# Nyström attention and expert layer in one kernel: the last 64 tokens of a batch stored in two transfers, and a new table of order, banks and warming

## The chip, the cores and the metric

The kernel runs on one core of a Trainium2 chip. The metric is the time of one execution on the device in microseconds (us). Before the change the median of 3 runs is 426.99 us, the lowest 425.55 and the highest 430.17. The core has five engines that work side by side and wait for one another through semaphores: PE (matrix multiply, with its weight loads as a row of their own, PEld), DVE (vector), ACT (scalar and activation), POOL (GpSimd) and SP, which here only issues transfers. [...]

## What is computed

Per batch (8) and head (8) of 576 tokens of width 64: attention through 32 landmarks. The landmarks are means of 18 neighbouring tokens.

```
q_lm = q.reshape(B, H, m, S // m, D).mean(axis=3)
k_lm = k.reshape(B, H, m, S // m, D).mean(axis=3)
A = sm(q, k_lm);  Bm = sm(q_lm, k_lm);  C = sm(q_lm, k)
Z = Bm^T / (norm1(Bm) * norminf(Bm) + 1e-06)
for _ in range(6):
    Z = 2 * Z - Z @ Bm @ Z
return A @ Z @ C @ v
```

The result, as 4608 rows of 512, goes to a layer of 8 experts with one expert per token (`sm` above is a softmax; a token's expert is the largest of 8 cosine scores):

```
h = np.maximum(x[mask] @ w1[e], 0.0)        # 512 -> 1024
out[mask] = gate_w[mask, None] * (h @ w2[e])  # 1024 -> 512
```

## The kernel before, in words

The kernel works batch by batch, and several batches are under way at once. For a batch b: `loads` and `load_values` bring K, Q and V; `sums` adds 18 tokens to a landmark (wholly on DVE, or half on POOL, L668, and half on DVE, L671); `inverse` makes Bm (its first matmuls, `ps<-ksum,qsum`, need the sums of K and Q; its first DVE step is L700) and `powers` iterates Z (`ek`); `values` makes C and C v; `queries` and `scored` make A with a softmax whose subtraction and division are done in `both`, either on POOL (L953) or on DVE (L955); its last steps are the transpose L938 and the split of A into two float16 parts, L941 on ACT and L943 on DVE. The attention output itself is never formed: `landmarks` makes W = Z C v, `first_weights` multiplies w1 by W (`ps<-wstage,wt`), `scaled` splits that product into two float16 parts (`ww`, L1389 and L1391), and `first` multiplies A by it (`ps<-ab,ww`), so that one matmul chain gives the hidden layer. `hidden` takes the maximum with 0 and splits into two float16 parts (`ht`, ACT L1442 and DVE L1444, 16 pairs per batch). `second` multiplies by w2 (`ps<-w2c,ht`), whose two parts `second_weights` makes (norm by L1405 on ACT or L1407 on DVE; the parts by L1430 on DVE or L1432 on ACT, and L1434 on DVE). `outputs` scales by the gate (L1535 on ACT or L1533 on DVE) and stores.

A batch has 576 = 4 x 128 + 64 tokens. For the last 64 (c = 4) the two halves of the 512 columns lie in the two halves of the 128 partitions of `yt`, and one transfer stores both (L1542). The other chunks are stored by L1540.

Which expert a batch's weights are loaded for is decided by `guess` and `choose` from the landmarks (the DVE steps end in `gi`), and SP reads that number (L1291) before it issues the loads of w1 and w2 (L1311). The whole batch uses one expert; a general path behind a branch covers the case in which a token disagrees.

The order is written out by hand. All these functions are generators that ask for an engine, a buffer or a PSUM bank at each step. `Weave.run` goes through the table `TURNS`: each pair of characters names the generator that makes its next step now, and so fixes the order of the instructions on every engine. `CHOICES` says, where a step may go to one of two engines, which one; `BANKS` names the PSUM banks; `WARM` says at which turns a number of matmuls on ones, in units of 128 columns, is put into PE's stream (`keep_warm`, L591, up to 512 columns each), whose result nobody reads. SP's queue is in the same order, and each of its entries waits for its data before the next is issued.

Of the kernel before, what the change touches and what calls it, by code (L numbers as in the profile page):

```python
# [53 lines left out]
BUFS = dict(k=2, q=2, v=2, ek=4, u=3, ec=2, ct=2, ae=3, at=2, st1=4, st2=4, w2=6, ww=2, ht=12, ab=3, yt=3, land=3, wt=3)  # L54

TURNS = (
    "000006060606060b0b353333060000333c003c0100000001010707080836360136010101343h3g3g34343h010101343434343434013i01"
# [4 lines left out]
    "021m1n1n4l4l4n2m2m2m1m1m1m4p382m4i4o4q1m1m4r4g4q4m4s4n4o4p4n4n2m2m1m0n0n0t0t2n2n4s4r4u2n2n4u4g4n1m1m1m4k2m4k4k"
    "4t2n594t1n1n2n4d4k0o0o4m391o1o4b4b1m1m1m0259395a2n022n025a391o1o3902021n1n0202020202021o1o2n2n4g2n2n2n1n1n394g"
    "2n1p1p1p40405b5g5g5a5h5h5b5b5b5g2n2n5g1p4d4d3a3a5b2n2n2n2n2n2n0o0o3a2n2n2n2n5a5h5h5g5g3a5h1o1o5k5h5g5g3a3a5k3a"
    "5h2n2n3b3b3b3b3b5l5l5l5l5b5b5h5b1r5k1r1r1r1r5k2n5l5l2n4v2n2n2n2n5l5l5l5l5h2n1r030303035b2n1p5b5b5l5j5j5b030303"
    "0303032n032n5b03035b5b03030303035c5c03030303035b4d4d5g5g5g031p4d5b5b5b2n5b1p1p5b5b5b5n5n5n41411r5n412n411r5p5p"
    "2n2n41415c5n5h5h2n5n5n5g5h2n5m5m2n5j0j0j5q5q5q1r1p1p1q5q5q1r5n415n1p2n5g5h415n5n5n2n5s5s2n2n5t5t1r5s1r41415t2n"
    "5n5n5n5n1r1r1r2o2o5u5u2o0k0k5w5n4w4w4w5n5n5n5w411r1r5v5n5z5z5n5n60605v2o2o2o2o2o61631r612o2o2o66666161615p6367"
    "5u415y5y5y672o656464686363635y5y68695y424y4y1r1r69422o2o654y4y1r420p0p6a6a422o4y4y2o2o6d6c6d422o6d436e6c6e6d43"
    "436f6d0u0u4y4y2o2o6h436h6h6h6h6h6h1t1t432p2p2p4y1t1t43431t1t1s1s4444443y2o6j4y2p2p4x444x2p1s1s2p386f1r1r4y1r6k"  # L70
    "6k2o2o6m6l6l6k442p6m53536i531t1t6l1s1s6k2o6r6i6l1w6j6p6p526l6q6q6k3b6l6g6s6t6n6n6n6n6r416n6k1w1w2p2p2p2p6l1u0z"
    "0z2p2p2p2p2p2p2p6l6t5m6s2p2p2p2p6n6k6k6k6k6k6k6n6n6s6s1s1s4y6l441w2p6k6o6l6l6t6t6t4y6s0u0u6n2p2p6n4z6n1w6u6u2p"
    "1u10102p2p2p2p2p2p1w1u2p4z4z4z6g6o6l6l4z1w501u1u503b0q0q2p2p2p2p7373731u506u506g1u50502p2p501u1v1w6o741u74516o"
    "77776o4v1u1w741u2p2p2p2p2p2p1w2p2p7c7c3b1w1w1w1w7d7d1w7c1w1w2p2p6o55557d551w54547f7f7g7g552q2q2q2q2q7g7b7b5510"
    "105515157l7l7l1w1w7l7l5535557t762q7u7t7e7e7t2q2q552q515151517x7x7i2q2q7t7t7t7t7v7u7j1y1y7h511y1y1x1x7w7x2q7w7y"
    "2q2q2q80767i7j777h7y2q2q2r2r7f76802q2r2q2q81442q827v7k822q2q817k851w86211x1x7k837z1x1x2q877z2r2r7k8483842r2r2r"
# [1555 lines left out]
```

## Time and profile before

| what | us |
|---|---|
| median of 3 runs (lowest, highest) | 426.99 (425.55, 430.17) |
| the profiled execution, its own time | 429.22 |
| its span, first to last instruction | 427.4 |
| PE matmuls busy | 403.5 (94%) |
| DVE busy | 343.2 (80%) |
| ACT busy | 242.2 (57%) |
| POOL busy | 72.6 (17%) |
| DMA, mean rate | 182 GB/s |

The share of busy time is a union over instructions. A matmul's end is modelled, and matmuls overlap, so PE at 94% isn't PE at its peak: a gap between two matmuls that is shorter than one matmul's latency doesn't show. The chain of waits, followed back from the last instruction, says which engine held the end up at each moment.

### The profile page before, as it was taken

To read this page: it belongs to the slowest core of one execution; us is meant where nothing else is said; L and a number is where in the kernel's file an instruction comes from. 1 tells how busy PE (TensorE), PEld (TensorE's weight loads), DVE (VectorE), ACT (ScalarE), POOL (GpSimd) and SP (SyncE) were. 2 spreads that over 40 slices of the span, in tenths; PEclk is the share of its full clock that TensorE was granted. 3 is DMA by queue.
4 is the path that set the end of the run, shared out by engine and by line. 5 is a ranking of instruction groups with operands and counts; after the bars stand their busy time and mean duration, and the time that the engine had idled before them with its cause. 6 is when DMAs were issued, how large, how long until landed. Compare 5 with 4: busy or idle time off the path is not lost.

```text
span 427.4 us, 14590 instructions
## 1 busy us (share of the span) xinstructions
PE 403.5 (94%) x6105; PEld 244.8 (57%) x6105; DVE 343.2 (80%) x1009; ACT 242.2 (57%) x536; POOL 72.6 (17%) x74
## 2 busy tenths in 40 slices
PE   8877999899999999999999899999999999999995
PEld 3344654467654665457665467556755576457644
DVE  5698999888898999987997669984898579788630
ACT  1258657548568554675588436755566577546311
POOL 5131243400121205201242132301110020000100
PEclk9999999999999999999999899999999999999999
DMA  8699394040599359273595249500187105741012
GB/s 313 245 320 391 121 354 164 22 168 15 186 350 380 132 176 355 82 280 120 183 350 192 101 154 364 193 3 29 53 288 292 58 28 180 276 168 51 2 58 73
DMA packets 23705, 77.67 MB, mean 182 GB/s; under 512 B 2768, under 2 KB 6096, under 8 KB 21840
## 3 DMA queue, kind: packets, MB, share of 16 engines
q1 hardware_dynamic: 23344, 76.49, 49.9%
q8 instruction: 49, 0.80, 0.7%
q10 hardware_dynamic: 288, 0.18, 0.2%
q14 instruction: 24, 0.20, 0.1%
HBM read 61.92 MB, written 14.75 MB: 179 GB/s over the span
## 4 chain that ended last, share of the span: by engine, by line
PE 55%; DVE 39%; issue 4%; ACT 1%; POOL 0%; DVEq 0%; ACTq 0%; POOLq 0%
PE ps L505 50%; DVE ht L1444 5%; DVE w2c L1434 4%; PE ps L591 3%; DVE ksum L671 2%; DVE qsum L671 2%; DVE asum L932 2%; DVE am L926 2%; DVE cm L813 2%; DVE ae L955 1%; DVE ae L919 1%; DVE ww L1391 1%; DVE w2c L1430 1%; DVE ab L943 1%; DVE wsq L1407 1%
## 5 line engine op out<-in xcount | busy, mean ns | idle before, releaser
L505 PE MATMUL ps<-w2c,ht 128*128 128x512 f16 (+2 forms) x1176 | 200.6, 342 | 1.1 <-DVE yt L1533 0.6
L505 PEld LDWEIGHTS <-ht 128*128 128x128 f16 (+1 forms) x1176 | 95.4, 102 | 82.4 <-issue 6.2
L505 PE MATMUL ps<-ab,ww 128*128 128x288 f16 x768 | 103.6, 286 | 2.2 <-DVE ht L1444 1.0
L505 PEld LDWEIGHTS <-ww 128*128 128x128 f16 x768 | 73.7, 98 | 27.4 <-issue 6.6
L1442 ACT ACTIVATE ht<-ps 128x288 f16<-128x288 f32 x128 | 47.3, 410 | 36.7 <-PE ps L505 36.2
L1444 DVE SCALAR_TENSOR_TENSOR ht<-ps,ht 128x288 f16<-128x288 f32 x128 | 53.3, 447 | 3.2 <-ACT ht L1442 3.0
L1434 DVE SCALAR_TENSOR_TENSOR w2c<-wstage,wsc,w2c 128x1024 f16<-128x1024 f32 x32 | 42.1, 1317 | 0.4
L1197 ACT ACTIVATE junk<-ps 128x512 bf16<-128x512 f32 (+1 forms) x40 | 23.8, 594 | 31.5 <-DVE lg L1194 30.1
L1535 ACT ACTIVATE yt<-ps,gfac 128x512 f32<-128x512 f32 (+1 forms) x32 | 19.9, 630 | 28.6 <-PE ps L505 24.8
L1326 ACT ACTIVATE junk<-wstage 128x1024 bf16<-128x1024 f32 x32 | 33.7, 1055 | 0.5
L1215 POOL TENSOR_TENSOR nrm<-ssq,half 128x5 f32<-128x5 f32 x8 | 9.6, 1194 | 130.5 <-ACT junk L1197 130.5
L668 POOL TENSOR_TENSOR half<-q_t 128x576 f32<-128x576 f32 x13 | 20.1, 1543 | 55.8 <-DVE ksum L671 22.3
L1405 ACT ACTIVATE junk<-wstage 128x1024 bf16<-128x1024 f32 x22 | 23.2, 1056 | 2.8 <-DMA wstage<-w 2.6
L668 POOL TENSOR_TENSOR half<-k_t 128x576 f32<-128x576 f32 x11 | 16.2, 1471 | 50.4 <-DMA k_t<-kT 37.4
L1432 ACT ACTIVATE w2c<-wstage,wsc 128x1024 f16<-128x1024 f32 x21 | 24.0, 1148 | 0.3 <-DVE wsc L1416 0.3
L1389 ACT ACTIVATE ww<-ps,wsc 128x1024 f16<-128x1024 f32 (+1 forms) x18 | 17.5, 1014 | 9.9 <-DVE wsc L1339 5.8
L953 POOL TENSOR_TENSOR ae<-ae,am 128x576 f32<-128x576 f32 x10 | 12.5, 1257 | 55.2 <-DVE am L926 55.2
L505 PE MATMUL ps<-ek 32*32 32x64 f32 (+1 forms) x768 | 16.4, 215 | 5.3 <-DVE ek L1012 2.3
L1194 DVE TENSOR_REDUCE lg<-ps 128x8 f32<-128x64 f32 (+1 forms) x40 | 8.7, 218 | 15.5 <-ACT junk L1197 9.5
L1391 DVE SCALAR_TENSOR_TENSOR ww<-ps,wsc,ww 128x1024 f16<-128x1024 f32 (+1 forms) x18 | 20.5, 1153 | 0.7 <-ACT ww L1389 0.7
L591 PE MATMUL ps<-ones 128*128 128x512 bf16 (+3 forms) x70 | 18.4, 411 | 2.4 <-POOL ones L523 1.7
L505 PEld LDWEIGHTS ps<-ek 32*32 32x32 f32 x768 | 11.7, 105 | 13.6 <-DVE ek L1012 6.0
(215 smaller groups left out, 526.5 us busy)
## 6 DMA issues: line engine op xcount, KB each, us to landing
wstage<-w SPq DMA_DIRECT2D x64, 512.0 KB, 8.1
v<-v SPq DMA_DIRECT2D x16, 512.0 KB, 4.8
k_t<-kT SPq DMA_DIRECT2D x7, 1152.0 KB, 10.1
q_t<-qT SPq DMA_DIRECT2D x7, 1152.0 KB, 5.9
out<-yt SPq DMA_DIRECT2D x31, 256.0 KB, 3.7
abs__137<-ab SPq DMA_DIRECT2D x8, 576.0 KB, 3.1
k_t<-kT SPq DMA_DIRECT2D x2, 576.0 KB, 4.0
q_t<-qT SPq DMA_DIRECT2D x2, 576.0 KB
```

Of the source, the lines that this page charges most:

```text
L505: pe.matmul(o, lhsT, rhs, start=start, stop=stop)
L591: pe.matmul(warmth[:, 0:k * P], ones16, bc(ones16.unsqueeze(1), [P, k, P]), start=True, stop=True)
L668: pool.tensor_tensor(out=half, in0=sv[:, :, :, 0:9], in1=sv[:, :, :, 9:18], op=ALU.add)
L1197: act.activation(junk[lo:hi, 0:512].rearrange("p (j g x) -> p j g x", j=4, g=2), pfv[lo:hi, :, n, :, 0:D], AF.Square, accum_out=ssq[lo:hi, ...
L1326: act.activation(junk, stage[1, b, q], AF.Square, accum_out=sq[:, q:q + 1])
L1391: vec.scalar_tensor_tensor(out=ww[:, 1], in0=pw, scalar=sc, in1=ww[:, 0], op0=ALU.mult, op1=ALU.subtract)
L1405: act.activation(junk, stage[2, b, q], AF.Abs, accum_out=sq[:, q:q + 1])
L1432: act.activation(w[:, 0], st, AF.Copy, scale=sc)
L1434: vec.scalar_tensor_tensor(out=w[:, 1], in0=st, scalar=sc, in1=w[:, 0], op0=ALU.mult, op1=ALU.subtract)
L1442: act.activation(ht[:, 0, r], ph[:, 0:HS], AF.Relu)
L1444: vec.scalar_tensor_tensor(out=ht[:, 1, r], in0=ph[:, 0:HS], scalar=0.0, in1=ht[:, 0, r], op0=ALU.max, op1=ALU.subtract)
L1535: act.activation(yt[:, 0:n], py[:, cols], AF.Copy, scale=fac)
```

## The change

Two things are changed. The store of the last 64 tokens is issued as two transfers of 64 rows of 256 columns. And the tables `TURNS`, `CHOICES`, `BANKS` and `WARM` are replaced; of these only `WARM` can be read.

```diff
-WARM = {1: 33, 19: 136, 36: 6, 46: 7, 108: 13, 126: 5, 134: 30, 192: 27, 225: 5}
+WARM = {4: 32, 23: 91, 59: 6, 79: 7, 153: 10, 190: 8, 211: 6}
...
         if c < 4:
             (act if last else sp).dma_start(out[t0:t0 + P, cols], yt[:, 0:n])
         else:
-            sp.dma_start(out[t0:t0 + 64].rearrange("t (s x) -> s t x", s=2), yt[:, 0:256])
+            for s in range(2):
+                sp.dma_start(out[t0:t0 + 64, 256 * s:256 * s + 256], yt[64 * s:64 * s + 64, 0:256])
```

The instructions stay the same but for the engine that `CHOICES` names, the stores and the warming. Counted in the order of instructions, before and after (two small copies, L877 and L1075, change by one each as well):

| step | before | after |
|---|---|---|
| softmax subtraction and division on DVE (L955) / on POOL (L953) | 13 / 19 | 6 / 26 |
| norm of w2 on DVE (L1407) / on ACT (L1405) | 10 / 22 | 6 / 26 |
| first part of w2 on DVE (L1430) / on ACT (L1432) | 11 / 21 | 8 / 24 |
| output of 512 columns on DVE (L1533) / on ACT (L1535) | 7 / 24 | 11 / 20 |
| C v on DVE (L855) / on ACT (L859, two each) | 6 / 4 | 3 / 10 |
| turned C, 512 columns, on DVE / on ACT (L874) | 5 / 11 | 3 / 13 |
| copies of the iteration, pairs of batches, on DVE (L1010) / on ACT (L1008) | 8 / 7 | 4 / 11 |
| warming matmuls, all sizes (L591) | 70 | 42 |

The first place is on PE, at the start of the program, where the warming run `ps<-ones_90` stands ahead of the first matmuls of `inverse(0)` (`ps<-ksum,qsum`) and of `values(0)` (`ps<-k_t,qsum`). Before, the run between `e_142` and `ksum,qsum` has 34 matmuls of 512 columns; its first and last rows:

```order
L505 MATMUL ps<-e_142,ones 128x64
L591 LDWEIGHTS ones_90
L591 MATMUL ps<-ones_90 128x512
...
L591 MATMUL ps<-ones_90 128x512
L505 MATMUL ps<-ksum,qsum 32x32 x8
L505 MATMUL ps<-k_t,qsum 32x288 x16
L591 LDWEIGHTS ones_90
L591 MATMUL ps<-ones_90 128x512
```

In the changed kernel the same run has 22 matmuls of 512 columns and one of 384:

```order
L505 MATMUL ps<-e_142,ones 128x64
L591 LDWEIGHTS ones_90
L591 MATMUL ps<-ones_90 128x512
...
L591 MATMUL ps<-ones_90 128x384
L505 MATMUL ps<-ksum,qsum 32x32 x8
L505 MATMUL ps<-k_t,qsum 32x288 x16
L505 LDWEIGHTS v_123
```

So the same matmuls stand behind 11.25 fewer warming matmuls of 512 columns, and the next short warming run, behind `k_t,qsum`, is gone.

The second place is on DVE, where the softmax of A for the second batch is made, among other steps. Before:

```order
L926 TENSOR_REDUCE am<-ae 128x18
L955 TENSOR_TENSOR ae<-ae,am 128x576
L836 RECIPROCAL cfac<-cfac 128x2
L839 TENSOR_TENSOR cfac<-cfac,rct 128x2
L1194 TENSOR_REDUCE lg_103<-ps 128x8
L671 TENSOR_REDUCE ksum<-half 128x64
L926 TENSOR_REDUCE am<-ae 128x18
L955 TENSOR_TENSOR ae<-ae,am 128x576
L932 TENSOR_REDUCE asum<-ae 128x18
```

In the changed kernel the subtractions of this softmax stand on POOL, between halves of the sums (`half`) and the power of the norms (`nrm`):

```order
L953 TENSOR_TENSOR ae<-ae,am 128x576
L668 TENSOR_TENSOR half<-k_t 128x576
L668 TENSOR_TENSOR half<-q_t 128x576 x2
L1215 TENSOR_TENSOR nrm<-ssq,half_115 128x5
L668 TENSOR_TENSOR half<-q_t 128x576
L953 TENSOR_TENSOR ae<-ae,am 128x576
L953 TENSOR_TENSOR ae<-ae,asum 128x576 x2
```

Two instructions of 576 elements have left DVE's stream here. In the stretch from the 13th to the 33rd `ht` of DVE (L1444) five such instructions and two of L1407 have gone in all, and none is left there.

The third place is on SP, around the first of the split stores. Before:

```order
L1540 DMA out<-yt 128x512
L1542 DMA out<-yt 2x64x256
L646 DMA v_123<-v 128x1024
L647 DMA v_123<-v 64x256
L633 DMA k_t<-kT 128x2304
```

In the changed kernel, in which the `dma_start` has moved down by one line:

```order
L633 DMA k_t<-kT 128x2304
L1543 DMA out<-yt 64x256 x2
L646 DMA v_123<-v 128x1024
L647 DMA v_123<-v 64x256
L1540 DMA out<-yt 128x512
```

The load of K has moved ahead of the store, and the store of a 128-row chunk behind it.

## Rows read from the trace of the kernel before

**Rows 1.** The page's first part: busy time, share of the span and instructions of each engine.

```profile
PE 403.5 (94%) x6105; PEld 244.8 (57%) x6105; DVE 343.2 (80%) x1009; ACT 242.2 (57%) x536; POOL 72.6 (17%) x74
```

**Rows 2.** The page's fourth part: shares of the span in the chain that ended last, by engine.

```profile
PE 55%; DVE 39%; issue 4%; ACT 1%; POOL 0%; DVEq 0%; ACTq 0%; POOLq 0%
```

**Rows 3.** Busy time in three stretches: from and to, length, then PE, PEld, DVE, ACT and POOL with their instructions, the granted clock of PE, the share of DMA and its rate.

```profile
60.00:85.00 25.00, 23.03 (x389) 11.39 (x387) 23.36 (x75) 14.58 (x32) 10.98 (x8) 1.00 0.33 117
...
119.00:157.00 38.00, 36.68 (x557) 21.47 (x556) 35.10 (x93) 25.75 (x56) 6.72 (x5) 1.00 0.75 273
...
283.00:424.00 141.00, 138.85 (x1868) 86.68 (x1852) 97.22 (x290) 72.72 (x157) 6.94 (x6) 1.00 0.33 117
```

**Rows 4.** Instructions in order of time at the start of the program, DVE and PE: start, duration, instruction, count, and in brackets the idle time before it and what ended it.

```profile
9.57 1.34 DVE L671 TENSOR_REDUCE qsum<-q_t 128x64 f32<-128x1152 f32 x1
14.68 0.23 DVE L700 TENSOR_REDUCE bm<-ps 128x2 f32<-128x64 f32 x1 [3.29 <-PE ps L505]
...
5.98 8.37 PE L591 MATMUL ps<-ones 128*128 128x512 bf16 x34
14.28 0.27 PE L505 MATMUL ps<-ksum,qsum 64*32 64x32 f32 x13
```

**Rows 5.** The same view near the end of the kernel: a run of matmuls of 512 columns with nothing between them.

```profile
403.84 6.21 PE L505 MATMUL ps<-w2c,ht 128*128 128x512 f16 x28
```

**Rows 6.** The same view, SP's last issue of the first V loads, and from the page's sixth part the median from issue to landing of such transfers (the last column).

```profile
4.80 0.49 SPq L647 DMA_DIRECT2D v<-v  x1
...
v<-v SPq DMA_DIRECT2D x16, 64.0 KB, 6.1
```

**Rows 7.** Instructions in order of time on PE ahead of the first matmuls of the expert layer (`ps<-ab,ww`).

```profile
36.90 1.63 PE L591 MATMUL ps<-ones 128*128 128x512 bf16 x7
...
38.66 0.91 PE L505 MATMUL ps<-ab,ww 128*128 128x288 f16 x6
```

**Rows 8.** Pieces of the chain that ended last, in order of time: start, duration, engine, tile and line.

```profile
68.77 0.76 DVE ae L955
...
71.28 0.76 DVE ae L955
...
78.05 1.14 DVE wsq L1407
...
121.40 1.35 DVE ae L955
...
128.15 0.77 DVE ae L955
...
130.22 0.67 DVE ae L955
131.00 1.13 DVE wsq L1407
```

**Rows 9.** Groups of instructions by line, engine and shape: count, busy time in all and mean ns of one, then the idle time before them and what ended it.

```profile
L1407 DVE TENSOR_REDUCE wsq<-wstage 128x1 f32<-128x1024 f32 x10 | 11.9, 1198 | 0.0
L1430 DVE TENSOR_SCALAR w2c<-wstage,wsc 128x1024 f16<-128x1024 f32 x11 | 8.9, 808 | 0.0
L955 DVE TENSOR_TENSOR ae<-ae,asum 128x576 f32<-128x576 f32 x7 | 5.8, 828 | 0.0
L955 DVE TENSOR_TENSOR ae<-ae,am 128x576 f32<-128x576 f32 x6 | 5.2, 869 | 0.1
L1533 DVE TENSOR_SCALAR yt<-ps,gfac 128x512 f32<-128x512 f32 x7 | 5.2, 740 | 0.1
L874 DVE COPY ct<-ps 128x512 f32<-128x512 f32 x5 | 3.4, 682 | 0.0
L1010 DVE COPY ek<-ps 128x128 f32<-128x128 f32 x8 | 2.3, 285 | 3.3 <-PE ps L505 3.3
...
L1405 ACT ACTIVATE junk<-wstage 128x1024 bf16<-128x1024 f32 x22 | 23.2, 1056 | 2.8 <-DMA wstage<-w 2.6
...
L953 POOL TENSOR_TENSOR ae<-ae,am 128x576 f32<-128x576 f32 x10 | 12.5, 1257 | 55.2 <-DVE am L926 55.2
```

**Rows 10.** A DVE instruction and a POOL instruction that overlap, in order of time; and all instructions of that DVE line, with the shortest, median and longest duration in ns.

```profile
43.19 1.82 DVE L943 SCALAR_TENSOR_TENSOR ab<-at,ab 128x576 f16<-128x576 f32 x1
...
43.09 1.30 POOL L668 TENSOR_TENSOR half<-k_t 128x576 f32<-128x576 f32 x1 [7.51 <-DMA k_t<-kT]
...
L943 DVE SCALAR_TENSOR_TENSOR ab<-at,ab x16: 733/748/1818, 37.7 to 380.4; 128x576 f16<-128x576 f32 x16
```

**Rows 11.** SP's issues of the two kinds of stores, shortest, median and longest in ns; the stretch in which one store of the last 64 tokens is the only traffic (columns as in rows 3); the one wait for a store on ACT, and SP's longest wait (us in total, times, longest).

```profile
L1542 SPq DMA_DIRECT2D out<-yt x8: 541/614/782, 98.0 to 413.9; - x8
L1540 SPq DMA_DIRECT2D out<-yt x32: 332/351/1527, 84.1 to 420.4; - x32
...
99.30:102.60 3.30, 3.30 (x64) 2.69 (x57) 3.17 (x8) 2.83 (x7) 0.00 (x0) 1.00 0.13 39
...
ACT yt L1535 <- DMA out<-yt: 2.9, 1, 2.9
...
SPq L1540 <- ACT yt L1535: 107.6, 10, 23.6
```

**Rows 12.** PE's longest wait that nothing in the profile explains, in order of time; and the stretch behind it (columns as in rows 3).

```profile
242.77 0.42 PE L505 MATMUL ps<-wgd,ab 32*128 32x72 f16 x29 [1.95 <-issue]
...
243.00:247.00 4.00, 4.00 (x35) 1.47 (x20) 1.40 (x5) 2.98 (x7) 1.58 (x2) 0.57 0.01 4
```

More of the change, by code (lines that the diff above doesn't have):

```diff
@@ L62 @@
[L62 to L76, printed above, removed]
@@ new lines @@
+    "33331i1i3q0101010101010101013h40360101013q3q0101423q42423y42364040404242421i1i1i1i4141414242424243433f3f001i1i"
+    "424141431j1j1k403f3f424242423y4141424242423z3f423z0d0d431k43413f424241431k37373737371k1l4941411l1k3z1l1k1m411k"
+    "3z49490e0e1k1k1k1k1l434b4b1j1j1j1j49493737414c4d4d020202434b3i3i1j1j3i4f1m2m2m4d1m3i431m4c2m2m0i0i43434f1m434h"
+    "1m3i3k3k3i3i1m371m2m2m4g4h4j0i0i1m1m1m1m434j3k1m1m4g3i3i2m2m2m2m4m2m2m4o024m374o1m4n4n4r4q4p1m1m0o0o4s4p1m022m"
+    "2m2m2m2m1n1n2m374v4v2m2m2m024w2n2n4w374x4x2n4u4r4q2n1m1m4r4r024i02024u1m4i4r4y4y4s4s4s4s4z2n3j4z2n023838504l1m"
@@ new lines @@
+    "1m4t50384t2m2m2n381m4k2m51513r4k38521n1n4t1o1o3l3l1n1n54545402522n531o1o1o1o53022n2n2n2n1p022n2n2n4t0254025402"
+    "0255551r02022n1r4i0202580o0o394i58585839584k2n5858582n582n39393958582n4k2n2n2n2n2n3954595839593a583a3a1p551p3a"
+    "3a1o1o5d59585858595d544l4l4l4l5d581n1n031r5d0303541r585858032n2n2n2n2n0303032n2n1r5d03031r1r5d555803035d03034l"
+    "5d032n2n035d5858031r5d1p1p0303030355032n03552n03033m3m5h551p55541r5d5e5e1p56565e5454553m5h5h5h565a5a55551p2n3m"
+    "3m5h5h5h3m1r1p1r5i2n542n5i0j0j5h5i1p1p555i5i0k0k2n1q1r1r1r3m545l5l551r5h3m2n2n5h5h5h1r1r3m5m5m2n2n2n2n2n2n2n2n"
@@ new lines @@
+    "5n5n5h5h5h5m5n5o5o3s3s3s5h5r2o2o5h5q5q5r5h5h5h3m5t2o5u5v5s2o2o5t1r2o5u5t5t0u0u5u5u5p5p5t5w5v5o1r1r2o2o5p5h3m5u"
+    "5w5x5p5p5h5h5z5z5s2o2o2o3m2o2o2o621r5p3a6361643u3u5x623n613n642o633u3u3n0p0p3n2o2o653u2o653u6769682o2o69673n69"
+    "68692p2p2p3o3o5a693u3u6b1r1r3u2p2p3o3o6a3o6b6b6b6b6b6b2o3o3o3p6c3j5l0q0q2p2p2p3t3t1t1t1s1s1s1s1t1t1s1s1r6a0t0t"
+    "3u6e6e2o2o3u2o6n6f6f6f6n6c5y6f6o6f6e6g6h6h3p6h6r6o3p6q6q6e3p3p6t6t6t2p2p2p2p2p2p2p6e6t6t6t1w6t6t2p0u0u2p2p2p2p"
+    "6e6t2p2p6s6e6r2p6e6e6f6x6p6f6x6t2p6f6t1u2p6s1s1s1u6e6e1w6u6u6f2p6e6x6x6s6s6s2p2p3u2p2p2p2p346p1t1t6f6f6p6e1u1u"
@@ new lines @@
+    "6x2p5y5y3v1u6u1u6p3v6p6p1w6f3v6w6w3v2p1u2p1t1t6f6j6j10106v3v0z0z746w376j1w3w3w1w2p6j70701u2p1w1u3w3w3w6v6v2p6j"
+    "6j3w7b2p1w1w1u1u1w1w2p7b7b7b7b6j3w6j7d1v6j1w7d2p2p2p2p2p2p2p2p2p2p1w1w1w1w1w1w7d1w3u7e7e7d7e7f7f7c7c7g7g7f1w1w"
+    "6i7d6i3x2q2q2q2q2q7j732q7m7d7h7h10107i7i7m2q2q2q2q2q2q3m0v0v7d1x1x7l1x1x3r1x1x7g7k7o7k7j3x737i2q2q7l7p7t7q737p"
+    "7h2q1w1w1w2r2r2r7u7q6j7c1y1y2q2q2q7w7r2r7v3a7n7t7i2q2q7x7n2q6j7y0w0w7o2r7r7u7v2q2q2r2q1z2r7n7x80707y817n3x7h7w"
+    "6j75757i803x3x3x1x1x1w811z218375042r2r2r2r2r862r2r7i8383832r041y1y8604041z2r040404878704041y1y832r2r2r2r898b7i"
@@ new lines @@
+    "3p1y1y2r2r04042r04040404048b851z042r2r83838383210404040404897i212r8b8b7i8b0416167h83837h047h7h8f8c8c898989201z"
+    "1z8f8f858888888f15158i218f8f8f8f3a2r7h1z1z7i7i1z1z2r852r8c7i21211z2r7h7h8p8p8f8f8f85858f8f7i2r2r212r8g8g8g7h21"
+    "2r8h8h2r217h2r218h8f8f2r8f212121216l21856l6l8f2s2s2s6l2r2r6l8q6l2r6l8f8f8f8f8s8s8e8e8e8r8f8f6k6k77772s2s778q8r"
+    "1b1b7721212r2r2r2r6k2r2r2r6k6k6m6m777721922r2r8u8u2r928s76929292777794949576939396968j8j8j952s98982121996m6m99"
+    "968e9b2t2t6m9c93952t9d952s2s2s9a6g97779595959a2s2s9b11119e9e9b9b9g9b1212942s2s2s9k9797949j9c22222t9k2s9j949g16"
@@ new lines @@
+    "162194772s2s949c9c9l94949c2s9n21219o97979f2323972s2s9n9494943x2s2s2s219o9p9p9f962s2t222222222222949r77779q9l9d"
+    "2t9d9m9r9s23239696969s8l8l2t2t8l8l8l232323238l9d9q2t2t2t2t2t9d9d9d969d2t9d3x9d2t2t2t1c1c2t2t962t2t2t2t26969624"
+    "242424249m9d9m269t249t242t9u9u78782t2t2t2t3p78243p2t249w9w7877789m249t2696969v9w9t9t8l268l252t8v269v2t2t24a16j"
+    "2626268l2626a1a1a1a2a2a29va3a32t2t2t2t9ua117171818a32679797979792t2u2u2t2t262626a1a1792t2u2679a8a8a98k9v8k8l8p"
+    "7aaaaa7a2t2t2t2t2t2t2t2t2626abab267aa7a73a26262t2t1c1c8w8waba4a48wa92727af8l2u2uafacacah74agag267a7aai8l2u2u2u"
@@ new lines @@
+    "ajakah2uamal2u2u272726262u2u2u2uakamaoanap262u2uaqapaaasad2uaaatan292v2v2828ao2vadalaaar2828abab2vas2u2uavaa2v"
+    "aqar272727272vakadadavaa29ata82u2u2u2u6mayazaxazaa282805ax1h1hak2v2v2v2b0505ajayabb005050505050505ai05abaaaaaa"
+    "ak29ajaj2b2v2v2v2v2v2vaa2va4ak05ak052828ajakab2v2v050505050505050505052v05292bb92929akabak29ak292b2b2b7a7aaeb9"
+    "b9b8b82vaab9ababaiaiai29b8abab2v2v2vac292v2v2vb9b9b9b92aae29b92bbcbcbbbbb9b9bdbdb92v2v2v2v2v2vaeae2bbcaeae2bbd"
+    "8mb92v2b2bbebe8m2v2v2b8m2v8m2v3x8mb9b9b92b2b8n8n8n2b8n8nb92v2w2w2wb9b9be2b2b7a7a8n8n2v2v8o8obg2bbhbhb98xb91d1d"
```

62 lines of the change are left out of this document (21 added, 41 removed).

## The prediction

> **What bounds the kernel now.** I read the shares of busy time first. PE is busy 403.5 of 427.4 us and DVE 343.2 [rows 1], but overlapping matmuls hide short gaps, so this names no bound. The chain of waits does: PE holds the end 55% of the span and DVE 39% [rows 2]. The stretches show where [rows 3]. From 60 to 85 and from 119 to 157 us DVE is busy 23.36 + 35.10 = 58.46 of 63 us, 93%: there DVE paces PE. From 283 to 424 it is busy 97.22 of 141, 69%, and PE 138.85: there PE is alone. Ahead of both lies the front, up to the first expert matmul at 38.66 us [rows 7], a string of short steps on all engines. So a step taken off DVE pays in the middle and not at the end, and a microsecond off the front pays whole, since all that follows starts earlier.
>
> **The warming run in front.** It has 34 matmuls and takes 8.37 us from 5.98 on. The first matmuls of the landmarks stand behind it and start at 14.28, though the last sums they need were done at 9.57 + 1.34 = 10.91; DVE waited 3.29 us for them [rows 4]. The changed run is shorter by 11.25 matmuls of 512 columns. One takes 6.21 / 28 = 0.222 us [rows 5], so the landmarks' matmuls start 11.25 x 0.222 = 2.5 us earlier, at 11.8, still behind the sums. What is late next could be V: its last transfer was issued at 4.80 and such ones land 6.1 us later in the median, at 10.9 [rows 6], before its reader at some 13 us. I take the whole 2.5 us. Above it, the last seven warming matmuls stand right ahead of the first expert matmul and take 1.63 us [rows 7]; the changed order keeps two at that place. DVE's part of that chain ends at nearly the same time, so I take nothing for it, with 1.6 us as the far end.
>
> **What leaves DVE for good in the middle.** Between the 13th and 33rd `ht` five instructions of L955 go to POOL and two of L1407 to ACT. All seven stood on the chain of waits: 0.76 + 0.76 + 1.14 + 1.35 + 0.77 + 0.67 + 1.13 = 6.58 us [rows 8]. If nothing took their place, that is the gain. If PE or the softmax, which now waits for POOL, became the limit at once, it is 0. DVE is at 93% there and PE not far behind it, so I take half, 3.3 us, between 0 and 6.6.
>
> In the rest of the kernel DVE gives up two more of L955 (0.85 us each), two of L1407 (1.20), three of L1430 (0.81), two of L874 (0.68) and four of L1010 (0.29), 9.0 us, and takes four outputs of 0.74 us, 3.0 us [rows 9]: 6.0 us less. DVE holds the end 39% of the span [rows 2], less towards the end [rows 3], so I take a quarter, 1.5 us, between 0 and 6.0. ACT takes over steps of 1.06 us for the norms [rows 9]; it is busy 57% of the span [rows 1] and 25.75 of 38 us in the worst stretch [rows 3], and this room hides them. Without it two norms in the middle would cost 2.1 us.
>
> **What POOL costs.** POOL makes seven more subtractions and divisions, of 1.26 us [rows 9] where DVE needs 0.85. And they hold DVE up: an L943 that overlapped a POOL instruction of 1.30 us took 1.82 us, against a median of 0.748 [rows 10]. So one collision costs up to 1.07 us, and seven between 0 and 7.5. Of the 16 instructions of that line the mean shows few such (the median is close to the shortest, 0.733), so I take one in five, 0.2 us each, 1.5 us in all.
>
> [...]
>
> **The split store.** One store took 0.614 us of SP to issue, a 128-row store 0.351 [rows 11]. Two of 64 rows cost between 0.35 (as one) and 1.23 us (twice the old); I take 0.7, so 0.1 us more each, 0.7 us for eight at SP. SP waited 107.6 us for outputs in 10 waits [rows 11], which hides it. While one such store ran alone the DMA engines were 13% busy, two of sixteen, at 39 GB/s for 3.3 us [rows 11]. Spread over more engines it would land sooner; the only wait for a store is 2.9 us on ACT [rows 11], at a place where PE goes on. I take 0, between -2.9 and +0.7 us.
>
> [...]
>
> **Stalls of PE that follow the order.** [...] I take 0, between -3.7 and +3.7.
>
> **The sum.** -2.5 - 3.3 - 1.5 + 1.5 = -5.8 us, against the profiled execution's own 429.22 us: 423.4. That execution is 2.2 us above the median of 426.99, a ratio of 0.9948; against the median the sum gives 421.2, and I say 421, 1.4% less.
>
> **The rivals.** (1) Only the front counts: DVE's place is taken by PE or by POOL's longer steps. PE being at 36.68 of 38 us in the second DVE stretch [rows 3] speaks for it, the seven pieces on the chain against it. 429.22 - 2.5 = 426.7, or 424.5 on the median's scale. (2) PE's clock falls in the front, where the new table has 9 instead of 25 warming matmuls between the first run and the first expert matmul. The drop behind the stall at 240.82 [rows 12] shows that a standstill of 1.95 us came before half rate. Two such drops of 1.7 us would give 423.4 + 3.4 = 426.8, so 424.6. [...] (3) POOL becomes the limit: each of the seven moved steps lies on the path, collides once (1.07 us) and lasts 0.41 us longer [rows 9, 10], 7 x 1.48 = 10.4 us, and no relief of DVE pays. 429.22 - 2.5 + 10.4 = 437.1, or 434.8, 1.8% slower. To be slower by 1% it takes 4.3 + 2.5 = 6.8 us, five of the seven. POOL's low share, 17% [rows 1], speaks against it. (4) The relief counts in full in the middle and by half in the rest: 429.22 - 2.5 - 6.6 - 3.0 + 1.5 = 418.6, so 416.4; DVE's 93% speaks for it.
>
> **How the numbers follow.** The forecast gets 0.48, with a range of its own from 417 to 424.5; rival 1 0.20, rival 2 0.12, rival 3 0.08, rival 4 0.12. The range from 413 to 428.5 reaches from rival 4 less its open ends (the 1.6 us in front, a stall that vanishes) to rivals 1 and 2 with a stall of 3.7 us more; rival 3 stays outside. A measurement of this kernel can tell about 1% from no change, that is 422.7 and 431.3. Faster: 0.41 of the forecast, rival 4, and 0.04 of rivals 1 and 2, 0.57. Slower: rival 3 and 0.02 for a pile of stalls, 0.10. The rest, 0.33, is no change.
>
> **What would show it.** Right: the landmarks' first matmuls start near 11.8 us and DVE's wait of 3.29 us ahead of L700 is under 1 us; the first expert matmul starts near 36; DVE's busy time is near 332 us (343.2 - 6.6 - 6.0 + 1.5) and the 33rd `ht` comes some 6 us earlier than before; stores of the last 64 tokens take clearly more than 13% of the DMA engines. Wrong: a granted clock under 1 between 12 and 40 us, waits for POOL of several us on DVE or ACT in the softmax, L943 or L1434 with a mean well above their medians, or an expert matmul that starts at 38 us or later.

## The result, and the profile after

The changed kernel takes 416.01 us (median of 4, 415.48 to 416.42) against 427.39 us (median of 4): 11.4 us less, a ratio of 0.9728 with a 95% interval of 0.9673 to 0.9783. On another occasion it gave 0.9715 (0.9673 to 0.9757). It is faster, by about twice what was forecast.

The first and fourth part of its page answer to [rows 1] and [rows 2]:

```profile
PE 396.3 (96%) x6077; PEld 243.4 (59%) x6077; DVE 329.4 (79%) x990; ACT 251.0 (61%) x555; POOL 79.0 (19%) x81
...
PE 69%; DVE 20%; ACT 3%; issue 3%; DMA 3%; POOL 1%; DVEq 0%; ACTq 0%; POOLq 0%
```

DVE lost 13.8 us of busy time, and its share of the chain fell from 39% to 20%, PE's rose from 55% to 69%. PE lost 7 us of busy time with 28 warming matmuls fewer. The 33rd `ht` of DVE comes at 149.07 us instead of 157.69. The front, in order of time on PE and DVE, answers to [rows 4] and [rows 7]:

```profile
5.87 5.32 PE L591 MATMUL ps<-ones 128*128 128x512 bf16 x23
11.12 0.27 PE L505 MATMUL ps<-ksum,qsum 64*32 64x32 f32 x13
...
30.70 2.81 PE L505 MATMUL ps<-wstage,wt 64*32 64x256 f32 x48
...
34.52 0.61 PE L591 MATMUL ps<-ones 128*128 128x512 bf16 x2
...
36.63 0.41 PE L505 MATMUL ps<-ab,ww 128*128 128x288 f16 x2
...
11.52 0.22 DVE L700 TENSOR_REDUCE bm<-ps 128x2 f32<-128x64 f32 x1 [0.25 <-PE ps L505]
```

The landmarks' first matmuls start at 11.12 (14.28 before), DVE's wait ahead of L700 is 0.25 us (3.29 before), the first expert matmul starts at 36.63 (38.66). So 3.2 us were won at 11 us and 2.0 are left at 37. What lies between shows in stretches (columns as in rows 3, granted clock third from the end):

```profile
16.00:20.00 4.00, 3.83 (x68) 1.20 (x66) 3.70 (x15) 1.69 (x5) 0.00 (x0) 0.58 0.78 243
28.00:32.00 4.00, 3.42 (x54) 1.67 (x61) 2.63 (x8) 2.31 (x5) 1.86 (x2) 0.50 0.97 327
32.00:36.00 4.00, 3.45 (x86) 1.65 (x71) 1.77 (x11) 1.78 (x5) 0.00 (x0) 0.79 1.02 385
36.00:40.00 4.00, 3.41 (x33) 2.25 (x34) 3.86 (x11) 3.94 (x8) 1.66 (x2) 0.64 0.89 374
```

In the profiled execution before, the clock was 1.00 in all of them. At 0.50 in the mean (30.70 to 33.51 us) 48 matmuls `wstage,wt` took 2.81 us; before, at 1.00, two runs of 32 took 1.10 and 1.09. With the last 16, 0.66 us, that is 3.47 instead of 2.19 us: against this one execution the fallen clock took 1.3 us back. It is not the change's alone. Two experiments further down, b_split and b_seven, leave the old front untouched, and there too the clock falls, to 0.50 from 36 to 40 us in b_split (the row) and from 20 to 24 us in b_seven; in b_split the same 64 matmuls took 1.96 and 1.96 us.

```profile
36.00:40.00 4.00, 3.89 (x53) 1.74 (x53) 3.58 (x11) 1.96 (x3) 1.16 (x1) 0.50 1.04 419
```

The two stretches in which DVE paced PE, and one of the length of the old tail, answer to [rows 3]:

```profile
60.00:85.00 25.00, 23.00 (x469) 12.09 (x468) 22.86 (x91) 15.54 (x37) 11.82 (x10) 1.00 0.45 150
119.00:157.00 38.00, 37.39 (x552) 23.86 (x551) 34.62 (x91) 29.26 (x63) 9.50 (x8) 1.00 0.70 262
270.00:411.00 141.00, 139.44 (x1888) 87.30 (x1885) 94.44 (x282) 75.68 (x163) 8.77 (x7) 1.00 0.33 116
```

DVE is still at 91% in the first two. PE runs 469 matmuls instead of 389 in the first and 552 instead of 557 in the second; the stretches are fixed in time, and the new order is further on in its work there.

Where the time went is read best from four marks on PE: the first, 241st and 385th of the 768 `ab,ww` matmuls, and the 1151st of the 1176 `w2c,ht`, nearly the last. The table has them for each profiled execution, with the experiments below; "standstill" is PE's waits that nothing in the profile explains, summed. A ratio is against runs of the kernel before that were taken beside it, slow executions of both left out, so it isn't the quotient of two medians of the table.

| kernel | median, us | ratio to before (95%) | first `ab,ww` | to 241st | to 385th | to 1151st `w2c,ht` | standstill |
|---|---|---|---|---|---|---|---|
| before | 427.39 | | 38.66 | 119.53 | 89.35 | 171.89 | 5.0 |
| b_split | 425.99 | 0.9986 (0.9946 to 1.0025) | 41.60 | 121.03 | 84.96 | 171.61 | 2.7 |
| b_short | 425.21 | 0.9937 (0.9897 to 0.9976) | 34.80 | 119.65 | 86.48 | 171.63 | 2.6 |
| b_seven | 426.46 | 1.0013 (0.9973 to 1.0054) | 38.29 | 119.48 | 85.35 | 171.73 | 2.6 |
| b_shift | 433.02 | 1.0138 (1.0085 to 1.0190) | 39.70 | 120.56 | 91.49 | 173.97 | 6.6 |
| b_engall | 438.30 | 1.0242 (1.0198 to 1.0286) | 39.56 | 124.05 | 89.60 | 175.18 | 3.2 |
| changed | 416.01 | 0.9728 (0.9673 to 0.9783) | 36.63 | 114.74 | 82.97 | 172.03 | 0.6 |
| a_same | 415.80 | 0.9715 (0.9673 to 0.9757) | 36.05 | 117.74 | 82.67 | 172.02 | 0.3 |
| a_unsplit | 418.31 | 0.9790 (0.9753 to 0.9827) | 38.01 | 115.50 | 82.98 | 172.28 | 1.7 |
| a_unsplit2 | 416.85 | 0.9736 (0.9691 to 0.9780) | 36.89 | 114.92 | 82.81 | 172.17 | 1.3 |
| a_long | 419.48 | 0.9839 (0.9808 to 0.9870) | 38.51 | 115.40 | 82.90 | 171.73 | 1.2 |
| a_seven | 419.54 | 0.9851 (0.9813 to 0.9889) | 36.46 | 117.66 | 81.80 | 171.87 | 0.0 |
| a_warm | 416.86 | 0.9769 (0.9731 to 0.9807) | 38.04 | 115.36 | 82.79 | 171.90 | 3.4 |
| a_engall | 440.71 | 1.0283 (1.0235 to 1.0331) | 37.99 | 122.38 | 94.51 | 177.75 | 0.5 |

One execution is not enough for a stretch: the changed kernel took 114.74 and 117.74 us to its 241st matmul in two of them. So take means over the executions in which nothing was edited that lies in the stretch. Front (before, b_split and b_seven; changed, a_same, the two with one store and a_seven): 39.5 to 36.8, 2.7 less. To the 241st (before, b_split, b_short; changed, a_same, both unsplit, a_long, a_warm): 120.1 to 115.6, 4.5 less. To the 385th (the same with b_seven and a_seven): 86.5 to 82.7, 3.8 less. The end: 171.7 to 172.0, 0.3 more. The sum is -10.7 us, and -11.4 were measured. The three executions of the old front lie 3.3 us apart, so a part is good to a microsecond or two and no better.

### The profile page after: what moved, and what is told of

The parts are those of the page before. It is cut to its first block, busy times and chain, and to the rows that moved or that the text cites. A ratio compares the mean times of both kernels' runs of the same rounds, so it can differ in the third digit from the quotient of the medians.

```text
span 414.4 us, 14573 instructions
## 1 busy us (share of the span) xinstructions
PE 396.3 (96%) x6077; PEld 243.4 (59%) x6077; DVE 329.4 (79%) x990; ACT 251.0 (61%) x555; POOL 79.0 (19%) x81
## 4 chain that ended last, share of the span: by engine, by line
PE 69%; DVE 20%; ACT 3%; issue 3%; DMA 3%; POOL 1%; DVEq 0%; ACTq 0%; POOLq 0%
PE ps L505 64%; DMA wstage<-w 3%; PE ps L591 3%; DVE ht L1444 2%; DVE w2c L1434 2%; DVE ae L919 1%; DVE cm L813 1%; DVE am L926 1%; ACT junk L1326 1%; PE ps L869 1%; POOL half L668 1%; DVE asum L932 1%; ACT junk L1197 1%; DVE qsum L671 1%; DVE lg L1223 1%
## 5 line engine op out<-in xcount | busy, mean ns | idle before, releaser
L505 PE MATMUL ps<-ab,ww 128*128 128x288 f16 x768 | 102.5, 288 | 0.6 <-DVE ww L1391 0.6
L1444 DVE SCALAR_TENSOR_TENSOR ht<-ps,ht 128x288 f16<-128x288 f32 x128 | 53.8, 446 | 4.8 <-ACT ht L1442 4.4
L1215 POOL TENSOR_TENSOR nrm<-ssq,half 128x5 f32<-128x5 f32 x8 | 10.6, 1326 | 131.4 <-ACT junk L1197 131.4
L1326 ACT ACTIVATE junk<-wstage 128x1024 bf16<-128x1024 f32 x32 | 33.7, 1053 | 1.3 <-DMA wstage<-w 1.0
L1535 ACT ACTIVATE yt<-ps,gfac 128x512 f32<-128x512 f32 (+1 forms) x28 | 17.2, 623 | 24.0 <-PE ps L505 17.5
L1432 ACT ACTIVATE w2c<-wstage,wsc 128x1024 f16<-128x1024 f32 x24 | 27.4, 1147 | 2.7 <-PE ps L505 2.0
L953 POOL TENSOR_TENSOR ae<-ae,asum 128x576 f32<-128x576 f32 x12 | 14.2, 1187 | 77.6 <-DVE asum L782 54.9
L1405 ACT ACTIVATE junk<-wstage 128x1024 bf16<-128x1024 f32 x26 | 27.5, 1056 | 1.5 <-DMA wstage<-w 1.0
L668 POOL TENSOR_TENSOR half<-q_t 128x576 f32<-128x576 f32 x13 | 18.9, 1455 | 34.8 <-DVE ksum L671 17.9
L953 POOL TENSOR_TENSOR ae<-ae,am 128x576 f32<-128x576 f32 x14 | 17.1, 1226 | 33.0 <-DVE am L926 20.9
L668 POOL TENSOR_TENSOR half<-k_t 128x576 f32<-128x576 f32 x11 | 14.3, 1298 | 36.1 <-DVE ksum L671 27.5
```

Source lines behind the costliest of these rows:

```text
L505: pe.matmul(o, lhsT, rhs, start=start, stop=stop)
L668: pool.tensor_tensor(out=half, in0=sv[:, :, :, 0:9], in1=sv[:, :, :, 9:18], op=ALU.add)
L953: pool.tensor_tensor(out=x, in0=x, in1=z, op=op)
L1326: act.activation(junk, stage[1, b, q], AF.Square, accum_out=sq[:, q:q + 1])
L1405: act.activation(junk, stage[2, b, q], AF.Abs, accum_out=sq[:, q:q + 1])
L1432: act.activation(w[:, 0], st, AF.Copy, scale=sc)
```

## The experiments

The names begin with b_ for an edit of the kernel before and a_ for one of the changed kernel. FLIP lists positions in `CHOICES` whose engine is changed to the other of the two.

**b_split.** The split store alone.

```diff
-            sp.dma_start(out[t0:t0 + 64].rearrange("t (s x) -> s t x", s=2), yt[:, 0:256])
+            for s in range(2):
+                sp.dma_start(out[t0:t0 + 64, 256 * s:256 * s + 256], yt[64 * s:64 * s + 64, 0:256])
```

> The kernel before with the split store alone. Relief theory (the gain of 11.4 us is the front, some 2 us, the steps taken off DVE, some 5 to 6, and standstills of PE that are gone, some 4): between -0.5 and +0.7 us against before, since SP has room for eight more issues and no engine waits for the store. Store theory (the split itself pays): -2 us or more, with the one wait for a store on ACT (2.88 us before) gone and the time following it. Both: the stretch in which such a store is alone shows more than 13% of the DMA engines busy.

Ratio 0.9986, no difference. The one wait for a store on ACT is still there, 2.2 us. The stretch in which the split store is the only traffic, here and in the changed kernel:

```profile
354.00:356.00 2.00, 2.00 (x19) 1.58 (x18) 2.00 (x5) 0.76 (x3) 0.00 (x0) 1.00 0.26 66
```

```profile
336.50:338.50 2.00, 2.00 (x18) 1.60 (x17) 2.00 (x3) 1.35 (x5) 0.00 (x0) 1.00 0.26 66
```

The DMA share is 0.26 at 66 GB/s where one store had 0.13 at 39 GB/s [rows 11]; 0.26 of 16 engines is 4.2, against 2.1, so more than two work on it. The wider spread brought nothing that can be measured: nobody waited for the old store but ACT once, for 2.9 us [rows 11].

**b_short.** The first warming run cut, alone.

```diff
-WARM = {1: 33, 19: 136, 36: 6, 46: 7, 108: 13, 126: 5, 134: 30, 192: 27, 225: 5}
+WARM = {1: 33, 19: 91, 36: 6, 46: 7, 108: 13, 126: 5, 134: 30, 192: 27, 225: 5}
```

> The kernel before with the first warming run cut from 136 to 91 units of 128 columns, nothing else. Relief theory: the first matmuls of the landmarks start at 11.8 instead of 14.28 us, the first expert matmul 2 to 2.5 us earlier than 38.66, and the time falls by about 2 us, to 425. Rival (the front is held by something else, or the granted clock falls behind the shorter run and takes it back): the first expert matmul stays within 0.7 us of 38.66 and the time within 1 us of before; a granted clock under 1 between 12 and 40 us would show it.

Ratio 0.9937, 2.7 us less (1.9 by the medians, against the 427.11 beside it); the interval lies wholly below 1. The landmarks' first matmuls start at 10.70 and the first expert matmul at 34.80. The clock was 0.64 from 16 to 20 us and 1.00 from 20 to 40, so with the old order's other warming runs the shorter one loses little.

**b_seven.** Five softmax steps of the middle to POOL and two norms of w2 to ACT, in the old order.

```diff
+FLIP = (43, 44, 49, 82, 87, 89, 90)
+CHOICES = "".join(str(1 - int(c)) if i in FLIP else c for i, c in enumerate(CHOICES))
```

> The kernel before with seven engine choices changed: five softmax steps of 576 elements between the 13th and 33rd ht from DVE to POOL, and two norms of w2 there from DVE to ACT; order, banks and warming as before. Relief theory: the 33rd ht (157.7 us before) comes 3 to 6 us earlier and the time falls by 3 to 6 us. Rival (the old order is fitted to the old engines; DVE only waits longer for POOL): the 33rd ht within 1.5 us, the time within 1.5 us of before or slower, with waits for POOL on DVE or ACT of several us.

Ratio 1.0013: nothing. The 33rd `ht` comes at 157.27 (157.69 before). The chain of waits shows why (pieces in order of time; the two added lines shift line numbers by 2):

```profile
67.71 0.66 DVE am L928
68.37 0.08 DVE cfac L838
68.45 1.16 POOL ae L955
69.61 1.51 issue
...
71.15 1.17 POOL ae L955
...
72.34 0.69 ACT ae L931
73.06 0.75 DVE asum L934
...
78.56 1.16 ACT junk L1407 x2
79.71 0.03 issue
79.74 0.16 DVE wsq L1412
```

The steps that stood on DVE at 68.77 and 71.28 [rows 8] stand at 68.45 and 71.15 on POOL, and the norm that was at 78.05 on DVE is at 78.56 on ACT. These three left DVE and not the chain. The four others, from 121 us on, did leave it, but PE took their place: it holds 59.5% of the chain from 119 to 157 us, against 14.8% before. The longest pieces there:

```profile
118.86 9.40 PE ps L507 x75
...
129.35 11.53 PE ps L507 x167
```

**b_shift.** The same columns of warming in twice as many matmuls, so that all later instructions of PE stand 34 matmuls later in its stream.

```diff
-        for i in range(0, n, 4):
-            k = min(n - i, 4)
+        w = 2 if n == 136 else 4
+        for i in range(0, n, w):
+            k = min(n - i, w)
```

> The kernel before, its first warming run made of 68 matmuls of 256 columns in place of 34 of 512: the same columns, and every later instruction of PE stands 34 matmuls later in PE's stream. Theory that the standstills of PE without a cause in the profile (5.0 us in 4, the longest 1.95 us at 240.8 with a fallen clock behind it) depend on where in the stream an instruction stands: the one in the wgd,ab matmuls near 240.8 shrinks under 0.7 us or moves elsewhere, and the time changes by -4 to +2 us. Rival (the standstill belongs to that run of small matmuls, whatever stands ahead of it): 1.5 to 2.4 us stand at the same matmuls again, the time within 1 us of before.

Ratio 1.0138, 5.9 us more than the 427.11 beside it. The `wgd,ab` matmuls run through at 248 us, but 57 us ahead of them, where PE had stood still for 1.22 us before (first row), it now does for 3.23 (order of time on PE, then the stretch behind it):

```profile
192.63 0.46 PE L505 MATMUL ps<-ek 32*32 32x64 f32 x17 [1.22 <-issue]
```

```profile
190.44 0.53 PE L505 MATMUL ps<-ek 32*32 32x64 f32 x22
194.19 0.41 PE L505 MATMUL ps<-ek 32*32 32x64 f32 x10 [3.23 <-issue]
...
192.00:197.00 5.00, 2.81 (x16) 1.12 (x17) 2.36 (x4) 0.92 (x1) 1.29 (x1) 0.76 0.21 75
```

The standstill stayed at its place in the stream, not with its work. Counted along PE's matmuls in the trace, the one behind the standstill of 1.22 us is the 2905th before, and the one behind that of 3.23 us is the 2905th in b_shift, though it is another `ek` matmul. At the 2905th b_split, b_short and b_seven stand still too, for 0.57, 0.38 and 1.09 us. How long a standstill is, or whether there is one, differs from one execution to the next: b_split has PE's stream unchanged, and there the run that stood still for 1.95 us [rows 12] is whole:

```profile
244.17 0.76 PE L505 MATMUL ps<-wgd,ab 32*128 32x72 f16 x70 [0.16 <-DVE ww L1391]
```

The standstills in b_shift sum to 6.6 us, against 2.6 to 5.0 in before, b_split, b_short and b_seven. Its trace is that of the longest of its six executions (435.86 us), and the standstills alone don't cover the 5.9 us that the median lost; the rest has no cause shown.

**a_unsplit** and, again beside **a_same**, **a_unsplit2.** The changed kernel with one store; a_same is the changed kernel itself.

```diff
-            for s in range(2):
-                sp.dma_start(out[t0:t0 + 64, 256 * s:256 * s + 256], yt[64 * s:64 * s + 64, 0:256])
+            sp.dma_start(out[t0:t0 + 64].rearrange("t (s x) -> s t x", s=2), yt[:, 0:256])
```

> The changed kernel with the last 64 tokens stored in one transfer again. Relief theory: within 0.7 us of the changed kernel (416.0). Store theory: 2 us or more slower, with a wait for a store on an engine or on SP that the changed kernel hasn't got.

> The changed kernel once more, beside the three others of this call and on their chip. What the first runs leave open is whether the changed kernel is really 2.3 us faster than the one with the unsplit store (416.0 against 418.3), since the trace of the latter lost its 2.2 us before its first store was issued. If that was chance of the chip or of PE's standstills, this run gives 416.5 to 419 and the next one the same within 1 us; if the split pays, 415.5 to 416.5 here and 2 us more there.

> The changed kernel with the store of the last 64 tokens in one transfer, again, on the same chip as the changed kernel. Store theory: 2 us or more slower than a_same. Theory of chance: within 1 us of a_same, and in the trace no engine later because of a store.

The first gave 418.31, 2.3 us above the changed kernel, but its trace was late by 1.4 us at the first expert matmul, some 60 us ahead of its first such store, so that much of the loss is not the store's. On one chip the pair gave 416.85 and 415.80, with intervals that overlap for the most part. No effect of the split is clear of the noise, which here would hide one of up to some 2 us.

**a_long.** The first warming run as long as before.

```diff
-WARM = {4: 32, 23: 91, 59: 6, 79: 7, 153: 10, 190: 8, 211: 6}
+WARM = {4: 32, 23: 136, 59: 6, 79: 7, 153: 10, 190: 8, 211: 6}
```

> The changed kernel with its first warming run at 136 units of 128 columns again, instead of 91. Relief theory: the landmarks' first matmuls start 2.5 us later, at 13.6, the first expert matmul 2 to 2.5 us later than 36.63, and the time is 418 to 418.5. Rival (the fallen clock of 0.58 at 16 to 20 us and of 0.50 to 0.79 at 28 to 40 us comes from the shorter run and eats its gain): the granted clock stays at 1 in these stretches, and the first expert matmul and the time come within 0.7 us of the changed kernel.

419.48, 3.5 us more; its interval doesn't touch that of the changed kernel. The changed kernel wasn't run beside a_long; against a_warm, which was, it is 2.6 us. The landmarks start at 13.83. The clock still falls, to 0.65 from 16 to 20 us and 0.72 from 32 to 36, so it is not the shorter run alone that makes it fall (nor the new order alone, as b_split and b_seven show).

**a_seven.** The seven steps back on DVE, in the new order.

```diff
+FLIP = (40, 42, 54, 82, 85, 88, 99)
+CHOICES = "".join(str(1 - int(c)) if i in FLIP else c for i, c in enumerate(CHOICES))
```

> The changed kernel with the seven engine choices of the middle as they were before: five softmax steps from POOL back to DVE, two norms of w2 from ACT back to DVE. Relief theory: the 33rd ht (149.1 us) comes 3 to 6 us later, and the time is 419 to 422. Rival (the new order brings the gain, whichever engine takes these steps): the 33rd ht within 1.5 us, the time 415 to 417.5.

419.54, 3.5 us more, and intervals apart; 2.7 us more than a_warm, which was run beside it. Its profiled execution, 417.78 us, was the shortest of its six, and it took 117.66 us to the 241st matmul, as a_same did (117.74), so the place of the loss isn't shown, only its size.

**a_warm.** More warming in the front's gaps.

```diff
-WARM = {4: 32, 23: 91, 59: 6, 79: 7, 153: 10, 190: 8, 211: 6}
+WARM = {4: 32, 23: 91, 45: 16, 59: 6, 79: 7, 100: 8, 120: 10, 133: 20, 148: 10, 153: 10, 190: 8, 211: 6}
```

> The changed kernel with 64 units of warming matmuls more in the front, in places where PE stood idle for 0.6 to 1.3 us (ahead of choose, three steps of the powers and the landmarks). If the fallen clock costs time in the front (64 matmuls wstage,wt took 2.81 + 0.66 us at 0.50, 2.2 us at full rate before): the granted clock is at 0.9 or more from 16 to 40 us, the first expert matmul starts 0.8 to 2 us earlier than 36.63 and the time is 414 to 415.2. Rival (PE has slack there, DVE and the loads of w1 set the pace): the first expert matmul within 0.5 us, the time within 0.7 us of 416.0.

416.86, no difference. The clock was 1.00 from 12 to 28 us and fell afterwards (0.92, then 0.65 from 32 to 36 us), behind a standstill of PE:

```profile
29.73 0.25 PE L505 MATMUL ps<-ek 32*32 32x32 f32 x5 [2.34 <-issue]
```

Behind it 48 `wstage,wt` took 2.74 us again. What a full clock would bring at that place stays open: no run here held it.

**a_engall and b_engall.** All choices but those of the landmark sums exchanged between the two orders; 89 of 250 differ. "Order" means `TURNS`, `BANKS` and `WARM` together here; no run tells them apart.

```diff
+FLIP = (
+    6, 15, 19, 28, 40, 42, 46, 47, 54, 57, 60, 67, 68, 71, 73, 74, 75, 76, 80, 82, 85, 88, 90, 91, 96,
...
+CHOICES = "".join(str(1 - int(c)) if i in FLIP else c for i, c in enumerate(CHOICES))
```

> The changed kernel (order, banks, warming, split) with 89 engine choices put back to those of the kernel before, all but those of the landmark sums. From first to 240th expert matmul the old order took 119.5 us with and without the seven moved steps, the new one 114.7 and with the seven steps put back 117.7. Theory that the new order and the engine choices only pay together: this stretch takes 118 to 121 us and the time is 419 to 424. Rival (the order pays by itself, the choices are worth only the seven): 117 to 118 us, 418 to 420.

> The kernel before with 89 engine choices taken from the changed kernel, all but those of the landmark sums; order, banks and warming as before. Theory that the choices pay only with the order: the stretch from the first to the 240th expert matmul takes 118.5 us or more and the time is within 2 us of before or slower, although DVE is some 13 us less busy. Relief theory, as it was in the prediction: the stretch falls to 116 us or less and the time by 4 us or more.

The new order with the old engines: 440.71, 2.8% slower than before (one of its six executions took 1371.53 us, which I can't explain; the median doesn't hang on it). The old order with the new engines: 438.30, 2.4% slower, although its DVE is busy 334.4 us, 8.8 less. Together they are 2.7% faster. Three of DVE's waits for ACT in b_engall, with those of the same steps before beneath (us in total, times, longest; line numbers are shifted by 7):

```profile
DVE lg L1201 <- ACT junk L1204: 12.4, 15, 1.3
DVE w2c L1441 <- ACT w2c L1439: 4.5, 4, 1.8
DVE ek L1019 <- ACT ek L1015: 4.4, 6, 1.8
```

```profile
DVE lg L1194 <- ACT junk L1197: 9.5, 13, 1.0
...
DVE ek L1012 <- ACT ek L1008: 0.4, 1, 0.4
```

All of DVE's waits for ACT sum to 41.3 us in b_engall, 18.6 before and 22.5 in the changed kernel. DVE's waits for PE went the other way, from 42.3 us before to 26.3. In a_engall it is PE that waits: its waits for DVE sum to 26.1 us, against 10.4 in the changed kernel. That a step which changes its engine has to be asked for at another turn is the reading I take from this; no run changed the turns of single steps.

## Why the prediction was right, and where it was not

It forecast 421 us, faster, and 416.01 came, inside the range. By its own steps:

**The front, -2.5 us: right.** The traces show -2.7 in the mean, b_short -2.7 (1.9 by the medians) and a_long 2.6 to 3.5 back. The 0.222 us for a warming matmul was a little low: the run itself took 8.37 / 34 = 0.246 [rows 4]. The clock under 1 between 12 and 40 us, a sign of being wrong by the prediction, is there in every trace of the new order (0.71 to 0.89 in the mean from 16 to 40 us). But it is there with the old front as well (1.00, 0.80 and 0.86 in before, b_split and b_seven), so how much of rival 2 is the change's is not shown; the 1.3 us, of the 3.4 that it asked for, are against the one execution that kept its clock.

**The steps off DVE in the middle, -3.3 us: right in size, by a guess between two ends.** Undoing the seven steps costs 3.5 us in the new order (2.7 against a_warm), and doing them in the old brings nothing; the stretch to the 241st matmul, in which they lie, won 4.5. The step that failed is to take half of their time on the chain because DVE was at 93%: the share of busy time doesn't say how much comes off the chain. In the old order both things happened that the prediction gave for its end at 0: three steps stood on the chain again, on POOL and ACT, and where the other four had been, PE held it. In the changed kernel the chain of the first stretch has no `ae` on POOL. So the new order puts other work of DVE between asking POOL and needing it; that this is what makes the difference is argued from the two chains, not tried by itself.

**The rest of DVE's relief, -1.5 us, and the standstills of PE, 0: the second was mis-sized.** From the 241st to the 385th matmul the kernel won 3.8 us, and nothing after it. Standstills are a part: in this stretch they took 3.2, 0.6, 1.8 and 1.1 us in the four traces of the old order (before, b_split, b_short, b_seven), 1.6 in the mean, and 0.3 us in one of seven with the new. In the whole kernel they were 5.0, 2.7 and 2.6 us in the three executions with PE's old stream (before, b_split, b_seven), 3.4 in the mean, against 0.8 over the five with the new one (changed, a_same, both unsplit, a_seven). The fallen clock behind the standstill of 1.95 us in before, 0.57 for 4.0 us [rows 12] and 0.50 from 244 to 246 us, is by estimate (1 - 0.57) x 4.0 = 1.7 us more, in one of the four. I had named the term, bounded it either way with the sum of these two, 3.7 us, and put it at zero, because the new order has the same small matmuls. Their neighbours don't tell the two apart: the `wgd,ab` matmuls of [rows 12] stand between long ones in both orders, first before, then in the changed kernel:

```profile
236.59 3.41 PE L505 MATMUL ps<-w2c,ht 128*128 128x512 f16 x15
...
243.12 4.45 PE L505 MATMUL ps<-w2c,ht 128*128 128x512 f16 x12
```

```profile
230.19 2.75 PE L505 MATMUL ps<-w2c,ht 128*128 128x512 f16 x12
232.88 0.87 PE L505 MATMUL ps<-wgd,ab 32*128 32x72 f16 x72
233.68 0.82 PE L505 MATMUL ps<-w2c,ht 128*128 128x512 f16 x3
```

At the 2905th matmul the old order has `ek` and stood still in all four traces; the changed kernel has `v,ct` there, and none of the seven traces of the new order stands still at that number. Why it is spared is open. With the standstills and the clock behind the one in before taken off, the old stretch took 84.3 to 84.7 us and the new 81.8 to 83.0. These last 1.8 us or so have the size of the -1.5 taken for the rest of DVE's relief, but no run ties them to it.

**POOL's price, +1.5 us: not found as a loss, though the collisions are there.** In the profiled execution of the changed kernel all 16 instructions of L943 lie between 741 and 767 ns, where one of [rows 10] took 1818. That is one execution: in a_same, the same kernel, one took 1656 (second row), and in a_unsplit2, a_long and a_warm 1447, 1872 and 1465, each beside a POOL instruction.

```profile
L943 DVE SCALAR_TENSOR_TENSOR ab<-at,ab x16: 741/748/767, 35.4 to 367.0; 128x576 f16<-128x576 f32 x16
```

```profile
L943 DVE SCALAR_TENSOR_TENSOR ab<-at,ab x16: 747/749/1656, 34.9 to 369.1; 128x576 f16<-128x576 f32 x16
```

Over all lines of DVE, every instruction that ran over 0.25 us longer than the median of its line and shape overlapped one of POOL: 15 before, with 10.5 us above the medians, and 10 in the changed kernel, with 7.6. So the sum fell by 2.9 us with seven instructions more on POOL; without the seven (a_seven) it is 5.6. L955 on DVE and L953 on POOL are now 6 and 26 instructions, and ACT waits 6.2 us for L953 in five places (3.8 before). Rival 3 is out. The 1656 ns in a_same, against a median of 749, show such a collision as [rows 10] did, and the change was faster all the same.

**The split store, 0: right**, as far as the noise lets one tell.

**The rivals.** Rival 4 (416.4) hit the number, by a reason that the runs refute: relief of DVE that counts in full would have shown in b_seven and b_engall. Rival 1 (DVE's place is taken at once, by PE or by POOL's steps) holds for the old order, where the seven steps bring nothing.

**What bounds the kernel now.** From the 385th matmul on all executions but b_shift and the two with 89 exchanged choices take 171.6 to 172.3 us, whatever was edited: that end is PE's. In the middle, the chain of the changed kernel runs once through a load of weights of 12 us. PE is busy without a gap meanwhile (12.00 of the 12.00 us from 118.7 on), and ACT waits only the last 0.26 us for it, so this isn't 12 us to be won:

```profile
118.39 0.35 DVE ht L1444
118.74 11.96 DMA wstage<-w
```

## What to carry to other kernels

A step that is moved from a busy engine to an idle one can be worth nothing until the order gives it time: look whether it comes back in the chain of waits on its new engine or another engine takes the chain over, and change the turn at which it is asked for together with the engine. Price such a table as a whole: its order and its engine choices were 2.8% and 2.4% slower apart and 2.7% faster together. Where single executions of a kernel differ by 1%, measure a stretch between fixed marks of the work over several of them before a microsecond in it is explained.

## What the runs showed of the hardware

PE's standstills without a cause in the profile came together with transfers on the queue that the page lists as `q8 instruction` (16 KB each; 49 of them in an execution of the kernel before, 0.80 MB in all). In each of the 24 standstills of over 0.5 us in the fourteen traces, such a transfer ended 1.2 to 1.6 us before PE went on. And 20 of the 24 fell on a few places of PE's stream, whatever work stood there: the 350th or 351st, 478th, 1372nd, 2905th and 3798th to 3800th matmul. The first two are 128 matmuls apart, as are the 3160th and 3288th, where b_shift stood still. What PE waited for there is not shown; no run changed the transfers themselves. The only traffic of note while PE stood still from 240.82 us in the kernel before was one of these (DMA view of 240 to 243 us: packets, MB, share):

```profile
q8 instruction: 1, 0.02, 1.8%
```

Ahead of that standstill 43 `wgd,ab`, matmuls of 72 columns, took 0.7 us. b_split ran through the same place with no standstill of this kind, so the place alone doesn't make one. The longest standstill was 3.23 us, in b_shift, where the DMA engines were busy with other transfers for 96% of the microsecond in which it began; the granted clock was 0.76 in the mean from 192 to 197 us, two of which PE still stood.
